# Handing out seven steps of the first weights' conversion in each early turn of an attention loop, not four

## The chip, the cores and the metric

The kernel runs on one core of a Trainium2 chip. The metric is the device time of one execution in microseconds (us). TensorE (PE in the profile) does matrix products and transposes, VectorE (DVE) and ScalarE (ACT) the elementwise work, GpSimd (POOL) a few additions, and SyncE (SP) issues the transfers between device memory and on-chip memory, all on one queue (q1).

## The reference

Three layers follow each other. The first is attention over q, k and v (2 batches, 8 heads, 576 positions, 64 wide), the sum of two softmax attentions: a pooled one, over means of four positions and repeated four times, and a local one with the mask |i - j| < 4. Its output is laid out as x, 1152 tokens by 512. The second is `g @ w_out` with `g = s * relu(x @ w_in)**2 + b`, 2048 wide; its weights arrive as float64 (1,024 KB for a quarter block of 128 x 1024 values). The third is a sum over four experts of `p[:, e] * (relu(x @ w1[e]) @ w2[e])`, 1024 wide, with normalised p.

    out = expert_layer(mlp(attention(q, k, v)))

## The kernel before, in words

**Units and turns.** Attention is cut into 16 units u (`NU`): four groups of (batch, half of the sequence) with four pairs of heads each. The loop at line 991 makes 19 turns i. Each turn calls eight functions (list at 979), each for the unit i minus a lag: `b_step` (lag 1: scores, maxima, exponentials), `a_step` (lag 0: transposes of k and q), `k_step`, `d_step` (lag 3: product with v), `c_step` (lag 2: transposes of the probabilities), `x_step` (lag 3: splits the result into a high part `xs[0]` and a low part `xs[1]`), `norm_step` (lag 1) and `v_step`. At a turn's end SP gets the loads: k and q for unit i+2 (lines 1021 and 1022), v4 and v for unit i. `unit u` is written u0, u1, ... below; unit u's scores are made in turn u+1.

**The first weights' conversion.** The first MLP's weights come as 64-bit words and are turned into two 32-bit parts, w0 and w1. For a quarter block these are six steps (line 207): `magnitude` (ACT, L157), `clamp` (DVE, L161), `join` (DVE, L167 and L175), `sign` (DVE, L186), `high` (ACT, L196) and `low` (DVE, L199), the last two after the next quarter's first steps have begun. `low` also issues the next raw load (L122) into one of two buffers. In turn 2 the four quarters of block 0 (24 steps) go into the list `side`: two of the first matrix, two of the second. They are called #1 to #4 here; #5 and #6, the first two of block 1, go into the list in turn 12. `side_step` takes one step from the list. The loop calls it after `b_step`, `k_step`, `c_step` and `v_step`; code that needs a quarter which isn't ready (`w1_ap`, `w2_ap`) calls it until it is.

**The dense products.** When a group's fourth unit is through `x_step` (u3 in turn 6), the first layer's products of that group go into `slots` and come out one or two a turn. All their matmuls have line 316.

**What sets the order.** The functions are called in the order of the text, but a scheduler then arranges each engine's instructions by readiness in its own model and by the order in which they were issued; only GpSimd keeps the text's order. On the chip every engine works its list in order. So the four matmuls of a dense product that need only the first pair of heads stand on PE in turn 4, long before the others. Where PE would idle in the first four units, `keep_warm` (L352) adds matmuls on zeros.

The functions that the change touches:

Of the kernel before, what the change touches and what calls it, by code (L numbers as in the profile page):

```python
# [22 lines left out]
def attn_moe_moe_kernel(  # L23
# [76 lines left out]
    def load_next():  # L100
        if not stream:
            return
        n, which, half = stream.pop(0)
        wi, wo, f0 = blocks[n]
        m = 2 if n < n_moe1 else 1
        dt = I32 if n < n_moe1 else F32
        if n < n_moe1:
            wi, wo = wi.bitcast(I32), wo.bitcast(I32)
        f0 += half * 256
        if which == 0:  # L110
            src = wi[:, f0 * m : (f0 + 256) * m].rearrange("(k p) f -> p k f", p=P)
        else:
            src = wo[f0 : f0 + 256, :].rearrange("(c p) d -> p c d", p=P)
        if n < n_moe1:
            t = rawp.tile([P, 2048], dt, tag="raw", name="raw")
        else:
            if "raw2" not in pools:
                t = rawp.tile([P, 2048], dt, tag="raw", name="raw2")
                pools["raw2"] = [t[:, :1024], t[:, 1024:]]
            t = pools["raw2"].pop(0)  # L120
            pools["raw2"].append(t)
        nc.sync.dma_start(out=t.rearrange("p (a b) -> p a b", a=src.shape[1]), in_=src)  # L122
        raw[n, which, half] = t
# [205 lines left out]
    def make_mask(t, m):  # L329
        if t == 0:  # L330
            nc.gpsimd.memset(mask, 0.0)
        off = t * TQ - window(t) if t <= MX else S - TQ - window(NTQ - 1)
        for sgn in (1, -1):
            nc.gpsimd.affine_select(
                out=mask[:, t : t + m],
                in_=mask[:, t : t + m],
                compare_op=ALU.is_ge,
                fill=NEG,
                base=FAC - 1 + sgn * off,
                pattern=[[0, m], [-sgn, W]],  # L340
                channel_multiplier=sgn,
            )
# [18 lines left out]
    def load_small():  # L361
        nc.sync.dma_start(out=s_sb, in_=s_in.rearrange("(o n) -> o n", o=1).to_broadcast([P, 1]))
        nc.sync.dma_start(out=b_sb, in_=b_in.rearrange("(o n) -> o n", o=1).to_broadcast([P, 1]))
        nc.sync.dma_start(out=pr, in_=probs.rearrange("(t p) e -> p t e", p=P))

    def norm_probs():
        nc.vector.tensor_reduce(out=prs, in_=pr, axis=AX.X, op=ALU.add)
        nc.vector.tensor_scalar(out=prs, in0=prs, scalar1=1e-9, scalar2=None, op0=ALU.add)
        nc.vector.reciprocal(out=prs, in_=prs)
        nc.vector.tensor_tensor(  # L370
            out=pr, in0=pr, in1=prs.to_broadcast([P, NT // P, E]), op=ALU.mult
        )
# [41 lines left out]
    def load_v4(u):  # L414
        if u < NU and unit(u)[3] == 0:
            g, j, b, hf = unit(u)
            v4 = ap4.tile([ND, 2, 2, FAC * D], F32, tag="v4", name="v4")
            nc.sync.dma_start(
                out=v4.rearrange("n a c f -> n (a c) f"),
                in_=v[b, 2 * j : 2 * j + 2].rearrange(  # L420
                    "a (c n r) d -> n (a c) (r d)", c=2, r=FAC
                ),
            )
            loaded["v4", u] = v4

    def load_k(u):
        if u < NU and unit(u)[3] == 0:
            g, j, b, hf = unit(u)
            kn = ap4.tile([KP, KR, 2, D], F32, tag="kn", name="kn", bufs=3)
            nc.sync.dma_start(  # L430
                out=kn, in_=k[b, 2 * j : 2 * j + 2].rearrange("a (p r) d -> p r a d", r=KR)
            )
            loaded["k", u] = kn

    def load_q(u):
        if u < NU:
            g, j, b, hf = unit(u)
            n0, m = tiles(hf)
            gd = m * TQ // FAC
            qn = ap2.tile([MX * TQ // FAC, FAC, 2, D], F32, tag="qn", name="qn")  # L440
            nc.sync.dma_start(
                out=qn[:gd],
                in_=q[b, 2 * j : 2 * j + 2, n0 * TQ : (n0 + m) * TQ, :].rearrange(
                    "a (n r) d -> n r a d", r=FAC
                ),
            )
            loaded["q", u] = qn

    def load_v(u):
        if u < NU:  # L450
            g, j, b, hf = unit(u)
            n0, m = tiles(hf)
            vn = ap2.tile([W, MX, 2, D], F32, tag="vn", name="vn", bufs=3)
            edge = 0 if hf == 0 else m - 1
            k0 = window(n0 + edge)
            nc.sync.dma_start(
                out=vn[:, edge],
                in_=v[b, 2 * j : 2 * j + 2, k0 : k0 + W, :].rearrange("a w d -> w a d"),
            )
            for a in range(2):  # L460
                t = 1 - hf
                s = v[b, 2 * j + a, window(n0 + t) :, :]
                nc.sync.dma_start(
                    out=vn[:, t : t + m - 1, a],
                    in_=bass.AP(s.tensor, s.offset, [[D, W], [TQ * D, m - 1], [1, D]]),
                )
            st["v", u] = vn
# [475 lines left out]
    def l1_steps(n, g):  # L943
        hs = hidden[n, g] = []
        if n < n_moe1:
            return [lambda fc=fc: moe1_l1(n, g, fc, hs) for fc in range(FC)]

        def run(half, i):
            if i == 0:
                hidden["steps"] = moe2_l1(n, g, half, hs)  # L950
            hidden["steps"][i]()

        return [lambda half=half, i=i: run(half, i) for half in range(2) for i in range(4)]

    def l2_steps(n, g):
        if n < n_moe1:
            return [lambda dc=dc: moe1_l2(n, g, dc, hidden[n, g]) for dc in range(KD)]
        t0, m = PARTS[g]
        return [
            lambda i=i: moe2_l2(n, t0 // P + i, i * P, hidden[n, g]) for i in range(2 * m // P)  # L960
        ]

    def side_step():
        if side:
            side.pop(0)()
        elif tail:
            tail.pop(0)()
# [23 lines left out]
    for i in range(last + 1):  # L991
        if i == 1:
            make_mask(CUT, 2)
            make_mask(MX + 1, 1)
        if i == 2:
            side += prep(0, 0, 0) + prep(0, 0, 1) + prep(0, 1, 0) + prep(0, 1, 1)
        if i == NU - 1:
            norm_probs()
        if i == NU - NP:
            rctx.close()  # L1000
            pools["wx"] = ctx.enter_context(
                tc.tile_pool(name="wx", bufs=1, side="right", reuse_waits="tile")
            )
            side += prep(1, 0, 0) + prep(1, 0, 1)
        for f, lag in steps:
            u = i - lag
            if 0 <= u < NU:

                with tc.high_priority(30) if f is a_step and u < NP else nullcontext():
                    f(u)  # L1010
            if f is x_step and u >= 0 and u % NP == NP - 1:
                slots += l1_steps(0, u // NP) + l2_steps(0, u // NP)
                if u < NP:

                    for _ in range(3):
                        slots.pop(0)()
            if f in (k_step, c_step) and slots and i < last:
                slots.pop(0)()
            if f in (b_step, k_step, c_step, v_step):
                side_step()  # L1020
        load_k(i + 2)
        load_q(i + 2)
        load_v4(i)
        load_v(i)
        if i == 4:
            load_small()
        if i < 2:
            load_next()
# [102 lines left out]
```

## Time and profile before

| what | value |
|---|---|
| runs | 702.38, 702.8 and 710.17 us, median 702.8 |
| span of the profiled execution | 709.2 us, first to last instruction |
| what lies around the span | not shown; the longest run is 1.0 above it |
| mean granted clock of the profiled execution | 0.969 |
| PE busy | 695.4 us, 98% of the span |
| DVE, ACT, POOL busy | 414.6, 347.8, 104.4 us |

The profiled execution's own time is not among the numbers; its span is 6.4 us above the median of the runs and 1.0 us below the longest, so it resembles the long one. Times of rows are from the span's start.

### The profile page before, as it was taken

The numbers are of one execution on the slowest core, as the hardware profiler recorded it, in microseconds if no ns is written. First come the engines' busy times: TensorE is split into PE (matmuls) and PEld (weight loads), VectorE is DVE, ScalarE is ACT, GpSimd is POOL, SyncE is SP. The second block draws the span as 40 slices with busy tenths as digits, with TensorE's granted clock in tenths as the row PEclk, the third lists the DMA queues.
The fourth block names the chain that finished last, engine by engine and source line by source line (L and its number), as shares of the span: only waits on it lengthen the run. The fifth ranks groups of instructions, "written<-read, shape, count | busy, mean of one in ns | idle before, by whom it ended". The sixth has DMA issues, their size and how long they took to land.

```text
span 709.2 us, 11407 instructions
## 1 busy us (share of the span) xinstructions
PE 695.4 (98%) x4496; PEld 633.9 (89%) x4496; DVE 414.6 (58%) x738; ACT 347.8 (49%) x854; POOL 104.4 (15%) x125
## 2 busy tenths in 40 slices
PE   8799989999999999999999999999999999999997
PEld 6678878899999999999989989899899898999996
DVE  3684987768894432579453555636645556365432
ACT  4553857768696565775454423423324244234220
POOL 5410244020000200103021021201210212010000
PEclk9855999999999999999999999999999999999999
DMA  9743644531540010200110110201102102011012
GB/s 182 197 116 95 119 85 105 132 125 63 175 146 34 1 30 0 60 2 30 30 61 30 60 30 30 64 27 60 60 30 60 30 31 64 26 56 35 1 55 79
DMA packets 54165, 46.39 MB, mean 65 GB/s; under 512 B 32224, under 2 KB 42720, under 8 KB 54112
## 3 DMA queue, kind: packets, MB, share of 16 engines
q1 hardware_dynamic: 54112, 45.67, 23.5%
q8 instruction: 35, 0.57, 0.3%
q14 instruction: 18, 0.15, 0.1%
HBM read 43.31 MB, written 2.36 MB: 64 GB/s over the span
## 4 chain that ended last, share of the span: by engine, by line
PE 88%; DVE 6%; ACT 3%; DMA 1%; issue 1%; POOL 0%; ACTq 0%; DVEq 0%
PE psm L316 41%; PE psx L864 25%; PE psx L316 13%; PE psa L598 2%; PE psa L686 2%; PE psa L658 1%; PE psa L352 1%; PE psa L616 1%; DMA qn<-in_q_dram 1%; PE psa L679 1%; PE psa L510 1%; DVE pd L636 1%; ACT pl L584 1%; DMA kn<-in_k_dram 1%; PE psa L492 1%
## 5 line engine op out<-in xcount | busy, mean ns | idle before, releaser
L316 PE MATMUL psm<-w,h 128*128 128x512 f32 x864 | 208.7, 391 | 0.0
L316 PEld LDWEIGHTS psm<-w,h 128*128 128x128 f32 x864 | 158.5, 188 | 30.0
L864 PE MATMUL psx<-x,w 128*128 128x320 f32 (+1 forms) x768 | 117.7, 296 | 0.0
L864 PEld LDWEIGHTS psx<-x,w 128*128 128x128 f32 x768 | 109.2, 189 | 1.7
L259 POOL TENSOR_TENSOR sw<-raw 128x256 f32<-128x256 f32 x32 | 31.3, 998 | 409.8 <-DMA raw<-in_moe_w_dram 292.0
L879 ACT COPY r<-psx 128x320 f32<-128x320 f32 (+1 forms) x96 | 38.1, 397 | 92.9 <-PE psx L864 92.5
L882 ACT ACTIVATE h<-r 128x320 fp32r<-128x320 f32 (+1 forms) x96 | 42.1, 444 | 83.5 <-DVE r L893 83.5
L935 DVE SCALAR_TENSOR_TENSOR acc<-psm,pr,acc 128x512 f32<-128x512 f32 x63 | 47.2, 749 | 57.9 <-PE psm L316 57.9
L864 PE MATMUL psx<-t,w 128*128 128x320 f32 (+1 forms) x448 | 80.2, 302 | 0.2 <-DVE r L893 0.2
L316 PE MATMUL psm<-x,w 128*128 128x320 f32 (+2 forms) x420 | 74.7, 329 | 4.6 <-ACT x L714 1.8
L893 DVE TENSOR_TENSOR r<-psx,r 128x320 f32<-128x320 f32 (+1 forms) x96 | 43.2, 456 | 58.3 <-PE psx L864 56.3
L316 PEld LDWEIGHTS psm<-x,w 128*128 128x128 f32 x420 | 67.6, 204 | 7.3 <-ACT x L714 2.1
L864 PEld LDWEIGHTS psx<-t,w 128*128 128x128 f32 x448 | 67.0, 188 | 4.5 <-DVE r L893 0.5
L883 DVE SCALAR_TENSOR_TENSOR h<-r,h 128x320 fp32r<-128x320 f32 (+1 forms) x96 | 48.1, 506 | 18.5 <-ACT h L882 16.4
L316 PE MATMUL psm<-h,w 128*128 128x256 f32 (+2 forms) x360 | 57.2, 305 | 0.5 <-ACT w L196 0.4
L316 PE MATMUL psx<-h,w 128*128 128x384 f32 (+1 forms) x312 | 55.8, 327 | 0.0
L316 PEld LDWEIGHTS psm<-h,w 128*128 128x128 f32 x360 | 50.8, 190 | 2.1 <-issue 1.1
L316 PEld LDWEIGHTS psx<-h,w 128*128 128x128 f32 x312 | 52.0, 188 | 0.0
L316 PE MATMUL psx<-x,w 128*128 128x384 f32 (+2 forms) x252 | 43.1, 320 | 0.0
L316 PEld LDWEIGHTS psx<-x,w 128*128 128x128 f32 x252 | 40.6, 188 | 0.0
L237 DVE TENSOR_TENSOR w<-raw,w 128x1024 fp32r<-128x1024 f32 x16 | 19.5, 1224 | 25.6 <-ACT w L234 25.6
L781 DVE TENSOR_TENSOR h<-r,h 128x384 fp32r<-128x384 f32 (+2 forms) x40 | 21.6, 541 | 19.9 <-ACT h L780 18.8
(109 smaller groups left out, 901.5 us busy)
## 6 DMA issues: line engine op xcount, KB each, us to landing
raw<-in_moe_w_dram SPq DMA_DIRECT2D x32, 512.0 KB
raw<-in_moe_w_in_dram SPq DMA_DIRECT2D x8, 1024.0 KB
raw<-in_moe_w_out_dram SPq DMA_DIRECT2D x8, 1024.0 KB
kn<-in_k_dram SPq DMA_DIRECT2D x8, 288.0 KB
v<-in_v_dram SPq DMA_DIRECT2D x8, 288.0 KB
out_dram<-acc SPq DMA_DIRECT2D x9, 256.0 KB
qn<-in_q_dram SPq DMA_DIRECT2D x8, 160.0 KB
vn<-in_v_dram SPq DMA_DIRECT2D x16, 72.0 KB
```

What stands on the lines that cost most here:

```text
L237: nc.vector.tensor_tensor(out=k0[1], in0=source(), in1=f32(k0[0]), op=ALU.subtract)
L259: nc.gpsimd.tensor_tensor(out=operand(out), in0=operand(x), in1=operand(y), op=op)
L316: nc.tensor.matmul(o, stat(ps, kk), mov(pm, kk, i), start=c == 0, stop=c == len(terms) - 1)
L598: nc.tensor.matmul(ps[0][:, t * W : t * W + W], qz[:, t].rearrange("p a q -> p (a q)"), kT[:, k0 : k0 + W], start=False, stop=t == m - 1,)
L686: nc.tensor.matmul(ps[o, t * TQ : t * TQ + TQ], vn[:, t, a], pT[:, i : i + TQ], start=True, stop=True,)
L781: nc.vector.tensor_tensor(out=h[1], in0=r, in1=f32(h[0]), op=ALU.subtract)
L864: nc.tensor.matmul(ps, s_ap(n, half, a, w, kk), xt[x, pi][b][:, kk], start=first and c == 0, stop=c == len(terms) - 1, skip_group_check=True,)
L879: nc.scalar.copy(t, st[name])
L882: nc.scalar.activation(out=h[0][:, halves[hf]], in_=t, func=ACTF.Relu)
L883: nc.vector.scalar_tensor_tensor(out=h[1][:, halves[hf]], in0=t, scalar=0.0, in1=f32(h[0][:, halves[hf]]), op0=ALU.max, op1=ALU.subtract,)
L893: nc.vector.tensor_tensor(out=st[t], in0=st[name], in1=st[t], op=ALU.add)
L935: nc.vector.scalar_tensor_tensor(out=a, in0=ps, scalar=p_e, in1=a, op0=ALU.mult, op1=ALU.add)
```

## The change

`side_step` is also called after `a_step`, `norm_step` and `d_step`, in the turns 0 to 6. The list is filled in turn 2, so up to seven steps leave it in each of the turns 2 to 5, and it is empty after the third step of turn 5; before, the last step left it in turn 7. No instruction of the computation is added or taken away.

```diff
-            if f in (b_step, k_step, c_step, v_step):
+            if f in (b_step, k_step, c_step, v_step) or (i < 7 and f in (a_step, norm_step, d_step)):
                 side_step()
```

What the scheduler makes of it shows on three engines. First DVE in turns 5 and 6; `cv` is a quarter's work buffer (before: cv_561 is #3; after: cv_466 is #3, cv_535 is #4), `qz1` the scaled q of u5, `md` a maximum of u4's pooled scores, `xg` the attention result of u2. Before:

```order
L618 TENSOR_REDUCE md_585<-psa_586 80x1
L199 TENSOR_TENSOR w01_286<-cv_399,w00_285 128x1024
L161 TENSOR_SCALAR cv_561<-cv_561 128x1024
L167 TENSOR_SCALAR cv_561<-cv_561 128x1024
L175 SCALAR_TENSOR_TENSOR cv_561<-raw_485,cv_561 128x1024
L524 TENSOR_SCALAR qz1_109<-psa_607 64x5x64
L539 TENSOR_REDUCE qd_614<-psa_607 128x80
L702 TENSOR_TENSOR xg_638<-psa_619,ud_636 128x256
L631 TENSOR_SCALAR sum0_106<-sum0_106 128x7
L186 SCALAR_TENSOR_TENSOR cv_561<-raw_485,cv_561 128x1024
```

and of the change:

```order
L618 TENSOR_REDUCE md_601<-psa_602 80x1
L161 TENSOR_SCALAR cv_466<-cv_466 128x1024
L167 TENSOR_SCALAR cv_466<-cv_466 128x1024
L175 SCALAR_TENSOR_TENSOR cv_466<-raw_404,cv_466 128x1024
L631 TENSOR_SCALAR sum0_106<-sum0_106 128x7
L186 SCALAR_TENSOR_TENSOR cv_466<-raw_404,cv_466 128x1024
L161 TENSOR_SCALAR cv_535<-cv_535 128x1024
L632 RECIPROCAL sum0_106<-sum0_106 128x7
L167 TENSOR_SCALAR cv_535<-cv_535 128x1024
L199 TENSOR_TENSOR w11_288<-cv_466,w10_287 128x1024
L175 SCALAR_TENSOR_TENSOR cv_535<-raw_495,cv_535 128x1024
L524 TENSOR_SCALAR qz1_109<-psa_623 64x5x64
```

Between the maximum and `qz1` stood four conversion instructions; now there are eight, and #2's L199 has moved ahead of the maximum.

Second SP, the loads at the end of turn 3; `raw` is a quarter (raw_404 is #3, raw_495 is #4), `qn` the q of u5. Before:

```order
L122 DMA raw_485<-in_moe_w_out_dram 128x2x1024
L441 DMA qn_487<-in_q_dram 80x8x64
L418 DMA v4_489<-in_v_dram 72x4x256
L456 DMA vn_491<-in_v_dram 72x2x64
L463 DMA vn_491<-in_v_dram 72x3x64 x2
```

and of the change:

```order
L122 DMA raw_404<-in_moe_w_out_dram 128x2x1024
L122 DMA raw_495<-in_moe_w_out_dram 128x2x1024
L441 DMA qn_497<-in_q_dram 80x8x64
L418 DMA v4_499<-in_v_dram 72x4x256
L456 DMA vn_501<-in_v_dram 72x2x64
L463 DMA vn_501<-in_v_dram 72x3x64 x2
```

Raw load #4, which waits for #2's L186 to free its buffer, now stands ahead of u5's q.

Third PE in turn 4, in one piece of the difference; x_76 is the high part of x, x_77 the low part, L610 the pooled scores of u3.

```order
 L316 MATMUL psm<-x_76,w_283 128x256 x2
-L316 MATMUL psm<-x_77,w_283 128x256 x2
-L316 MATMUL psm<-x_76,w_284 128x256 x2
-L610 MATMUL psa<-kd_435,qd_111 128x144
+L610 MATMUL psa<-kd_442,qd_111 128x144
+L316 MATMUL psm<-x_77,w_283 128x256
+L316 MATMUL psm<-x_76,w_284 128x256
+L316 MATMUL psm<-x_77,w_283 128x256
+L316 MATMUL psm<-x_76,w_284 128x256
 L510 MATMUL psa<-ident,qn 128x80 x4
```

u3's pooled scores no longer stand behind the matmuls that need the low part.

## Rows read from the trace of the kernel before

**Rows 1.** Stretches of the span: busy us of each engine, granted clock, transfers.

```profile
0.00:30.20 30.20, 25.31 (x188) 18.16 (x188) 15.94 (x39) 16.50 (x55) 13.31 (x30) 1.00 0.96 196
30.20:71.20 41.00, 38.81 (x215) 31.98 (x215) 24.39 (x50) 18.16 (x62) 6.81 (x7) 0.50 0.42 110
71.20:105.40 34.20, 31.70 (x310) 27.65 (x309) 30.66 (x57) 25.66 (x90) 13.36 (x13) 1.00 0.55 106
105.40:108.80 3.40, 3.40 (x15) 3.23 (x15) 1.17 (x5) 1.90 (x11) 0.08 (x1) 0.50 0.47 129
...
135.00:300.00 165.00, 165.00 (x1120) 162.72 (x1120) 101.99 (x157) 113.31 (x233) 10.84 (x11) 1.00 0.21 69
```

**Rows 2.** PE in order of time, turns 4 to 7: start, us, instruction, idle before.

```profile
29.96 0.55 PE L316 MATMUL psm<-x,w 128*128 128x256 f32 x2 [0.89 <-ACT x L714]
31.46 1.22 PE L316 MATMUL psm<-x,w 128*128 128x256 f32 x4 [0.94 <-POOL x L716]
...
42.61 2.07 PE L316 MATMUL psm<-x,w 128*128 128x256 f32 x8
45.93 1.22 PE L316 MATMUL psm<-x,w 128*128 128x256 f32 x4 [1.25 <-DVE w L199]
46.95 0.73 PE L510 MATMUL psa<-ident,qn 80*128 80x80 f32 x4
...
52.87 2.41 PE L598 MATMUL psa<-kT,qz 128*128 128x72 f32 x10
...
67.79 4.30 PE L316 MATMUL psm<-x,w 128*128 128x256 f32 x21
```

**Rows 3.** DVE in order of time, turns 4 to 6.

```profile
29.39 0.30 DVE L636 TENSOR_TENSOR pd<-pd,sum 128x144 f32<-128x144 f32 x1
...
42.76 1.39 DVE L636 TENSOR_TENSOR pd<-pd,sum 128x144 f32<-128x144 f32 x1
44.07 0.29 DVE L618 TENSOR_REDUCE md<-psa 80x1 f32<-80x144 f32 x1
44.29 1.58 DVE L199 TENSOR_TENSOR w<-cv,w 128x1024 fp32r<-128x1024 f32 x1
48.50 0.49 DVE L524 TENSOR_SCALAR qz<-psa 64x320 f32<-64x320 f32 x1
```

**Rows 4.** Conversion instructions by line, to 130 us: shortest, median, longest ns.

```profile
L161 DVE TENSOR_SCALAR cv<-cv x6: 674/687/1223, 22.2 to 90.2; 128x1024 f32<-128x1024 f32 x6
L167 DVE TENSOR_SCALAR cv<-cv x6: 676/690/1040, 23.6 to 92.0; 128x1024 int32<-128x1024 int32 x6
L175 DVE SCALAR_TENSOR_TENSOR cv<-raw,cv x6: 1209/1226/1330, 24.4 to 92.7; 128x1024 int32<-128x1024 int32 x6
L186 DVE SCALAR_TENSOR_TENSOR cv<-raw,cv x6: 1173/1217/1556, 25.7 to 95.2; 128x1024 int32<-128x1024 int32 x6
L199 DVE TENSOR_TENSOR w<-cv,w x6: 1206/1216/1582, 29.6 to 129.5; 128x1024 fp32r<-128x1024 f32 x6
```

**Rows 5.** SP's issues in order of time: start, us, transfer.

```profile
40.40 0.38 SPq L122 DMA_DIRECT2D raw<-in_moe_w_out_dram  x1
```

**Rows 6.** The whole span's chain in order of time: start, us, what.

```profile
17.51 6.06 DMA qn<-in_q_dram
```

**Rows 7.** DVE's groups by line, 72 to 110 us: count, busy us, mean ns.

```profile
L186 DVE SCALAR_TENSOR_TENSOR cv<-raw,cv 128x1024 int32<-128x1024 int32 x3 | 3.9, 1315 | 0.0
...
L199 DVE TENSOR_TENSOR w<-cv,w 128x1024 fp32r<-128x1024 f32 x2 | 2.4, 1216 | 0.1
```

**Rows 8.** PE in order of time, turns 8 to 11: what it waited for.

```profile
79.48 0.50 PE L316 MATMUL psm<-h,w 128*128 128x256 f32 x2 [0.41 <-ACT w L196]
...
97.18 1.00 PE L316 MATMUL psm<-x,w 128*128 128x320 f32 x5 [0.58 <-POOL x L716]
...
99.17 0.51 PE L610 MATMUL psa<-kd,qd 128*128 128x144 f32 x2 [0.32 <-DVE ml L606]
```

**Rows 9.** The chain from 85 to 100 us, shares by line.

```profile
by line: DVE cv L186 17.1%; issue 11.6%; DVE pd L636 11.1%; DVE pl L633 10.0%; DVE w L199 7.6%; PE psa L598 7.0%; DVE ml L606 5.6%; DVE qd L531 5.4%; PE psm L316 5.0%; DVE cv L161 4.0%; DVE md L618 3.6%; PE psa L610 3.5%; DVE xg L702 3.3%; 
```

## The prediction

> **What bounds the kernel now.** I first read the busy times by stretch [rows 1]. From 135 to 300 us PE is busy in all 165.0 us, and later nearly so; a step that leaves this work alone can change the time only by what PE loses before 135 us. That loss has two kinds. Idle: 4.9 us before 30.2, 2.2 us from 30.2 to 71.2, 2.5 us from 71.2 to 105.4. And clock: from 30.2 to 71.2 us the granted clock is 0.50, the lower level, 1.2 GHz, and again for 3.4 us from 105.4. PE had been busy 25.3 of 30.2 us when it fell, and was in a run of 21 dense matmuls when it rose [rows 2]. In that slow stretch PE is the bound: 38.8 of 41.0 us busy, DVE only 24.4. From 71.2 to 105.4 it is close: PE 31.7 and DVE 30.7 of 34.2. The order of time [rows 2, 3] then tells which instruction PE or DVE stands at, and the chain [rows 9] what is late in the second stretch.
>
> **What is added and removed.** Nothing: 24 conversion steps before and after, with the same DMAs. They leave the list up to two turns earlier. That the edit changes nothing is excluded, since the lists above differ on PE, DVE and SP.
>
> **Turn 4.** #1's L199 now runs ahead of u0's `xg`, so x comes one L199 later, 1.22 us [rows 4]. PE, which waited 0.89 us for it already, gets to its first two dense matmuls 1.22 us later, at 31.18. L610 goes next and no longer stands behind the low part of x; the four matmuls behind it follow at once if that part takes as long as its mean, or wait on. Bounds for PE at L510 of u4: +0.4 with the 0.94 us wait for the low part hidden behind L610's half microsecond, +0.9 with none of it. I take +0.65, between them; nothing in the rows is nearer to one.
>
> **Turn 5.** #2's L199 moves ahead of L633, L636 and the second L618. Before, PE waited 1.25 us for it between eight and four dense matmuls [rows 2]; now it is done some 1.3 to 1.6 us after the first L618, while PE is still in the eight. That wait goes: -1.25. PE's L510 of u5 stands at 46.95 + 0.65 - 1.25 = 46.35.
>
> **Turn 6, the cost.** The price is on DVE, ahead of `qz1` (L524). The second L618 ended at 44.36 [rows 3]; in the change it waits for +0.65 and for L199, 1.22 to 1.58, so it ends near 46.5 (46.2 to 46.6). Then come, by the medians of [rows 4]: L161 0.69, L167 0.69, L175 1.23, L186 1.22 for #3, L161 0.69 and L167 0.69 of #4, L199 1.22 of #3, L175 1.23 of #4, and two of L631 and L632 that I estimate at 0.2 each. Sum 8.06 us, to 54.56, and L524 itself 0.49: 55.05. The matmuls of u5's scores (L598) need it. PE would be there 52.87 - 46.95 = 5.92 us after L510, at 52.27. It waits 2.8 us, and starts 2.2 us later than before (52.87). Bounds: L636 took 1.39 us here and 0.30 a turn earlier [rows 3]; at 0.30 the cost is +1.1. With the longest durations of [rows 4] for all eight, 2.7 us more in sum, it is +4.8. I take +2.1, near the medians; L636 comes at nearly the same time as before, so its 1.39 is the nearer row.
>
> The raw load #4 and, behind it, u5's q are on SP: #4 is freed by #2's L186, which ended just before 40.40 [rows 5]. u5's q is issued about 0.4 us later. An earlier q load that was issued right behind a raw load took 6.06 us in the chain [rows 6], so this one lands near 46.9, 0.5 us after PE wants it. That is hidden: PE has 2.8 us to spare before DVE lets it go on.
>
> [...]
>
> The other loads that stand behind #4, #5 and #6 (v4 and vn of u3, later q and vn of u6 and u7) are used a turn or more later, and I cost them at nothing; that cover is PE's slow turns of some 12 us, and it shrinks where the clock is high.
>
> **Turns 6 and 7.** From there PE's list is as before, and DVE has slack again (24.4 of 41.0 us busy). PE arrives at the 21 dense matmuls at 67.79 + 2.1 = 69.9.
>
> **Turns 8 to 11, the gain.** Before, #4, #5 and #6 were converted between 71 and 97 us: three each of L161, L167, L175 and L186, and two of L199 [rows 7], by the medians of [rows 4] some 14 us of DVE. #4 is now done by turn 6 and #5 half done, so about 8 us leave that stretch. The chain runs through just these lines [rows 9] (L186 17.1%, L199 7.6%, L161 4.0%). But PE worked on meanwhile, and only its idle time can come back. The waits that end on conversion or on DVE's lateness are 0.41 (#4's L196), 0.58 and 0.32 [rows 8]: 1.3 us. The rest of the 2.5 us ends on latency between engines and I leave it. The 3.4 us of half clock from 105.4 cost 1.7; I leave them too. Bounds: nothing comes back, 0, or all of it, 2.5 + 1.7 = 4.2.
>
> **The sum.** +2.1 - 1.3 = +0.8 us. Against the profiled execution that is a span of 710.0. But that execution is a long one, 6.4 us above the median of 702.8. I put the sum on the median: 703.6, 703.5 in round numbers. With the bounds of the two terms, +1.1 - 4.2 = -3.1 to +4.8 - 0 = +4.8, it is 699.7 to 707.6. What makes executions of before differ by 7.4 us the rows don't show; the nearest that could is the half-clock stretch, where 7.4 us are 15 us of half clock.
>
> **Rivals.**
> *The clock helps (chance 0.25).* The wait between the eight and the four dense matmuls is what goes, so twelve run unbroken, 3.3 us. If this brings the clock back in turn 5, and DVE still holds PE until 55, PE's 15 us from 55 to 70 run at full clock and give back up to 7.5 us. For: the clock came back in a run of 21, and again at 108.8 us with PE busy in all of 105.4 to 108.8 [rows 1]. Against: the 2.8 us wait that follows lets it fall again, and the short executions may have had this gain before. With them at the median, what is left is the gain of turns 8 to 11 at its upper end: 702.8 + 1.1 - 4.2 = 699.7; with both, about 697.
>
> *The q load is late (0.10).* If u5's q takes twice the 6.06 us, it lands at 53, PE waits 6.6 us at L510 and reaches the scores at 58.9 instead of 52.87: +6.0 - 1.3, 707.5. It decides once q lands after 49.2, when the 2.8 us are used up. Against: 1 MB and 160 KB took the 6.06 us.
>
> *The clock hurts (0.20), the slower side.* The 2.8 us wait in turn 6 stands right before the nine dense matmuls of that turn. Where the clock came back there in the short executions, it no longer does, and most executions are of the long kind: 710.2 + 0.8 = 711. It decides when PE idles over 2 us ahead of L598 with the clock at either level. For: at 30.2 us the clock fell after a stretch with PE idle for 4.9 us in all. Against: I see no short execution.
>
> **The numbers.** Forecast 0.45, rivals 0.25, 0.10, 0.20. The time is that of the forecast, 703.5. The forecast's own range is 699.7 to 707.6; down to 697 and up to 711 it takes in most of the rivals, and about 2 in 10 lie outside. 2%, about what a measurement of this kernel can tell from no change, is 14 us: below 688.7 or above 716.9. No case ends there alone; below, the helpful clock together with every bound, 0.03; above, the long kind with a longer half-clock stretch as well, 0.06.
>
> **What would show it.** In the profile of the change: PE waits 2 to 3 us ahead of u5's L598 for DVE (right) or not at all (the cost is wrong); no wait for #2's L199 among the dense matmuls of turn 5; conversion instructions of #4 gone from 70 to 81 us; PE idle of 71 to 105 us down from 2.5 to about 1.2. The forecast is wrong if the half-clock stretch has another length than 41 us plus 2, or if new ones appear: each 2 us of it count as 1.

## The result and the profile after

| | before | after |
|---|---|---|
| median of 20 runs each | 702.97 us | 707.28 us |
| lowest and highest | 698.62, 712.49 | 705.43, 711.52 |
| ratio after to before | | 1.0088, 95% interval 1.0070 to 1.0106 |
| span of the profiled execution | 709.2 | 707.1 |

The change costs 4 to 6 us: 4.3 us, 0.6%, between the medians, and 0.9% by the ratio, which leaves out executions more than 1.5% above the fastest of their kernel. That is within 2% and within the range by 0.3 us, 3.8 us above the forecast. The two profiled executions, read alone, say the opposite: the one of after is 2.1 us the shorter. That contradiction is what the experiments had to solve.

The stretches of the profile after (start and end, length, busy us of PE, PEld, DVE, ACT and POOL with counts, granted clock, busy share of the DMA engines and GB/s) answer to [rows 1]:

```profile
0.00:30.20 30.20, 25.14 (x186) 18.00 (x186) 16.08 (x38) 16.07 (x54) 13.51 (x29) 1.00 0.93 199
30.20:50.70 20.50, 19.67 (x118) 16.50 (x119) 15.62 (x27) 12.63 (x38) 6.40 (x6) 0.50 0.39 113
50.70:54.10 3.40, 0.95 (x7) 0.48 (x5) 3.34 (x5) 0.37 (x1) 0.00 (x0) 1.00 1.09 309
54.10:74.60 20.50, 19.94 (x101) 16.61 (x101) 14.12 (x29) 10.61 (x35) 1.56 (x1) 0.50 0.64 118
74.60:105.40 30.80, 30.00 (x306) 26.86 (x306) 22.14 (x51) 22.26 (x89) 10.43 (x13) 1.00 0.34 75
105.40:108.80 3.40, 3.40 (x45) 3.04 (x43) 3.00 (x7) 3.10 (x11) 1.11 (x2) 1.00 0.50 134
```

The clock comes back at 50.7 us, 20 us earlier than in the profiled execution of before, and finds PE standing still: 0.95 us busy of 3.4. It falls again, for another 20.5 us. So the half-clock time is 41.0 us, as in the one long stretch of before, but in two pieces, and the dip of 3.4 us at 105.4 is gone.

PE after, in order of time (start, us, instruction, count, idle before it and what ended that), answers to [rows 2]:

```profile
30.97 0.80 PE L316 MATMUL psm<-x,w 128*128 128x256 f32 x2 [2.03 <-ACT x L714]
...
32.90 0.73 PE L510 MATMUL psa<-ident,qn 80*128 80x80 f32 x4
...
42.55 2.93 PE L316 MATMUL psm<-x,w 128*128 128x256 f32 x12
45.54 0.80 PE L510 MATMUL psa<-ident,qn 80*128 80x80 f32 x4
...
53.71 2.08 PE L598 MATMUL psa<-kT,qz 128*128 128x72 f32 x10 [2.45 <-DVE qz L524]
```

The 1.25 us wait between eight and four dense matmuls is gone (x12 unbroken), and 2.45 us stand ahead of u5's scores instead. DVE after, answering to [rows 3], shows where they come from:

```profile
42.19 1.21 DVE L199 TENSOR_TENSOR w<-cv,w 128x1024 fp32r<-128x1024 f32 x1
...
43.91 0.30 DVE L618 TENSOR_REDUCE md<-psa 80x1 f32<-80x144 f32 x1
44.12 0.68 DVE L161 TENSOR_SCALAR cv<-cv 128x1024 f32<-128x1024 f32 x1
...
51.92 1.21 DVE L175 SCALAR_TENSOR_TENSOR cv<-raw,cv 128x1024 int32<-128x1024 int32 x1
53.16 0.49 DVE L524 TENSOR_SCALAR qz<-psa 64x320 f32<-64x320 f32 x1
```

From 44.12 to 53.13 us DVE has nothing but the eight conversion instructions of #3 and #4 and two small ones; then comes L524. SP after, answering to [rows 5]:

```profile
26.82 13.06 SPq L122 DMA_DIRECT2D raw<-in_moe_w_out_dram  x2
39.94 0.60 SPq L441 DMA_DIRECT2D qn<-in_q_dram  x1
```

SP stands 13 us at the second raw load (#4), and u5's q goes out behind it, at 39.94. Before, u5's q went out right behind raw load #3, 12.95 us ahead of #4 [rows 5]:

```profile
26.96 0.39 SPq L122 DMA_DIRECT2D raw<-in_moe_w_out_dram  x1
27.45 0.60 SPq L441 DMA_DIRECT2D qn<-in_q_dram  x1
```

### The profile page after: what moved, and what is told of

It is laid out like the page before. It is cut to its first block, busy times and chain, and to the rows that moved or that the text cites. A ratio compares the mean times of both kernels' runs of the same rounds, so it can differ in the third digit from the quotient of the medians.

```text
span 707.1 us, 11409 instructions
## 1 busy us (share of the span) xinstructions
PE 693.3 (98%) x4496; PEld 632.9 (89%) x4496; DVE 414.8 (59%) x738; ACT 348.4 (49%) x854; POOL 102.4 (14%) x125
## 4 chain that ended last, share of the span: by engine, by line
PE 91%; DVE 5%; ACT 2%; issue 1%; POOL 0%; ACTq 0%
PE psm L316 42%; PE psx L864 25%; PE psx L316 13%; PE psa L598 2%; PE psa L658 2%; PE psa L686 2%; PE psa L352 1%; PE psa L616 1%; PE psa L679 1%; PE psa L510 1%; PE psa L492 1%; DVE cv L161 1%; DVE w L199 0%; PE psa L589 0%; DVE ts L836 0%
```

## The experiments

**What every run tells.** Each run lists its span and mean granted clock, so its half-clock time can be worked out as 2 x (1 - clock) x span. Against the stretches read from the traces this is off by up to 2 us (15.5 against 13.6 us in `after_warm8`). The profiled execution of before gives 44 us. That number is used below.

**1. Before again, and parts of the change.** `same` is the kernel before, to catch a short execution. `six` and `five` leave calls out:

```diff
-            if f in (b_step, k_step, c_step, v_step) or (i < 7 and f in (a_step, norm_step, d_step)):
+            if f in (b_step, k_step, c_step, v_step) or (i < 7 and f in (norm_step, d_step)):   # six
+            if f in (b_step, k_step, c_step, v_step) or (i < 7 and f is d_step):                # five
```

Expected of `same`:

> The kernel before, unchanged, to see one of its short executions. Theory 1 (eight conversion instructions ahead of unit 5's qz, and PE's 2.45 us wait there, are the loss) and theory 2 (#1's L199 ahead of unit 0's xg is the loss) say only that its median is near 703. Theory 3 (the clock): if the profile catches an execution of about 700 us, its half-clock stretches before 135 us sum to some 26 to 31 us instead of the 41.0 + 3.4 us of the 709.2 us span, and the clock comes back around turn 5 or 6 and doesn't fall again; if the sum is 41 us or more in a short execution, theory 3 is wrong.

Of `six`:

> Steps are handed out also behind norm_step and d_step, not behind a_step: #1's L199 still runs ahead of unit 0's xg and #2's L199 early, as in the change, but only three conversion instructions (L161, L167, L175 of #3) stand ahead of unit 5's qz, not eight. Theory 1: PE's 2.45 us wait for L524 is gone or under 0.5 us, and the median is 700 to 703. Theory 2: the 2.03 us wait for x in turn 4 stays and the median stays at about 707. Theory 3: the clock does not fall again in turn 6, some 27 to 38 us at half clock, 699 to 704.

Of `five`:

> Steps are handed out also behind d_step alone: #2's L199 is early, #1's L199 stays behind unit 0's xg as before, and no clump stands ahead of unit 5's qz. Theory 1: no wait for L524, the 1.25 us wait in turn 5 is gone, 701 to 702. Theory 2: the same 701 to 702, since turn 4 is as before; so if six is at 707 and this one at 702, theory 2 holds, and if both are near 702, theory 1. Theory 3: as six, 699 to 704, with some 27 to 38 us at half clock.

Measured: `same` 701.12 us; `six` 701.98 us, ratio to before 1.0020 (0.9989 to 1.0052); `five` 702.35 us, 1.0031 (1.0017 to 1.0046). `five` ran once more under the label five_warm8 (its keep-warm matmuls are four, in spite of the label): 703.33 us.

> Steps handed out also behind d_step alone, once more, one look: as in the first run of it, half clock of 20 to 28 us in two stretches, about 702.

Its half-clock time came in three stretches, 23.8 us in all, not in two.

The profile of `same` caught a short execution, span 701.1 us. Its stretches:

```profile
28.70:52.60 23.90, 21.89 (x125) 17.70 (x125) 16.48 (x27) 11.50 (x38) 6.78 (x7) 0.50 0.54 141
52.60:97.00 44.40, 41.55 (x398) 35.91 (x398) 38.18 (x79) 31.85 (x114) 12.99 (x14) 1.00 0.56 118
97.00:100.40 3.40, 3.40 (x14) 3.04 (x15) 1.36 (x4) 1.56 (x10) 0.71 (x1) 0.50 0.36 94
```

Here too the clock comes back in turn 6, at 52.6 us, but PE is in u5's scores then and has no wait above 0.42 us until 72: it stays up for 44 us. So the two kinds of executions of before differ by the clock: of 47 (12 of `same`, 35 of before beside it) 35 have 7 to 27 us of half clock, with a median time of 700.9 us, and 12 have 44 us, with 710.3. Per microsecond of half clock that is 9.5 / 27 = 0.35 us, less than the half that PE alone would lose; that a faster PE waits more would explain it, but was not tried. All 20 executions of after have 30 to 42 us: the short kind is gone. `six` has 24 to 31 (27 to 38 expected), `five` 21 to 28.

The clock doesn't tell the whole time. Three of the 35 take 709 us with 21 us of half clock. And in after three executions with 31 us take 711 us, the longest of all, while those with 41 to 42 us take 707 to 709. No profile caught one of these, and what makes them longer is open.

Theory 2 falls: `six` keeps the 2.03 us wait for x in turn 4 and is 5 us faster than the change. What `six` lacks is the clump ahead of L524:

```profile
31.72 0.51 PE L316 MATMUL psm<-x,w 128*128 128x256 f32 x2 [2.03 <-ACT x L714]
...
46.84 1.23 DVE L175 SCALAR_TENSOR_TENSOR cv<-raw,cv 128x1024 int32<-128x1024 int32 x1
48.10 0.49 DVE L524 TENSOR_SCALAR qz<-psa 64x320 f32<-64x320 f32 x1
...
49.33 1.33 PE L598 MATMUL psa<-kT,qz 128*128 128x72 f32 x10
```

L524 starts 5.06 us earlier than in the change, and PE does not wait for it. `six` lacks the late load as well, so it can't tell the two apart: u5's q goes out ahead of raw #4.

```profile
28.07 0.60 SPq L441 DMA_DIRECT2D qn<-in_q_dram  x1
39.71 0.39 SPq L122 DMA_DIRECT2D raw<-in_moe_w_out_dram  x1
```

**2. More keep-warm work in units 0 to 3.**

```diff
-    fill = [4 if u < NP else 0 for u in range(NU)]
+    fill = [8 if u < NP else 0 for u in range(NU)]
```

As `before_warm8` and, with the change, `after_warm8`:

> The kernel before with eight keep-warm matmuls, not four, in each place of units 0 to 3: PE has less idle time up to 30 us. Theory 3: the clock falls later than 30 us or comes back earlier than 71 us, and the time falls by half of what the half-clock stretch loses: 10 us less of it gives 5 us, about 698, less the keep-warm matmuls' own time where PE is the bound (some 160 more rows of matmuls). Theories 1 and 2 expect no gain from it: 703 to 706, the keep-warm work being only added.

> The change with eight keep-warm matmuls, not four, in each place of units 0 to 3, as the run before_warm8 had them, whose median was 698.2 with 4 us of half clock in most executions. Theory 3: with the clock up in turns 4 and 5, PE comes to unit 5's scores earlier and waits 4 us or more for the eight conversion instructions; either the clock falls there (some 10 to 20 us of half clock, 701 to 706), or it stays and what is left is idle time, 698 to 700. Theory 1 without the clock: 2 to 3 us above before_warm8, 700 to 701. If the handing out as such were good once the clock is high: 697 or less.

Measured: `before_warm8` 698.24 us, ratio 0.9964 (0.9932 to 0.9996), half clock 0 to 14 us, median 4, with 80 keep-warm matmuls more (168 for 88); `after_warm8` 706.29 us, half clock 7 to 24, median 17 (5.1 above the median of the before beside it; the ratio, 1.0026 with 0.9983 to 1.0069, takes in no change, so the traces are compared). Useless matmuls make before faster; with them, the change costs 8 us between the medians. Stretch 27 to 75 us of both, before first:

```profile
27.00:75.00 48.00, 45.63 (x451) 39.02 (x450) 42.10 (x88) 35.63 (x128) 12.93 (x11) 1.00 0.66 150
```

```profile
27.00:75.00 48.00, 43.30 (x367) 35.64 (x368) 41.72 (x76) 30.82 (x104) 11.72 (x9) 0.86 0.66 152
```

Between the profiled spans, 704.4 and 696.5, lie 7.9 us. The half clock is 13.6 us in the one and 3.4 in the other, worth 5.1 at most; PE's idle time is 2.3 us more in this stretch. PE's waits after (27 to 75 us: in total, times, longest) show one that the profile of the change did not have:

```profile
PE psa L510 <- DMA qn<-in_q_dram: 2.2, 1, 2.2
...
PE psa L598 <- DVE qz L524: 0.6, 1, 0.6
```

With the clock up, PE is at L510 of u5 before the q load has landed. The 4 us or more that were expected ahead of L598 are 0.6, since PE has lost 2.2 at the transposes before it.

**3. Filling the wait.** Twelve more keep-warm matmuls right ahead of u5's scores (`after_fill`), or behind u6's transposes (`after_late`):

```diff
-            keep_warm(ps, n, fill[u])
+            keep_warm(ps, n, 16 if u == 3 and not cols else fill[u])   # after_fill
-        keep_warm(psq, m * TQ, fill[u])
+        keep_warm(psq, m * TQ, 12 if u == 6 else fill[u])              # after_late
```

> The change, with twelve more keep-warm matmuls of 128x256 right ahead of unit 5's scores, where PE waits 2.45 us for L524. The lists of DVE, SP and POOL are those of the change, and L524 comes at the same time. Theory 3 (PE's idle time in turn 6 lets the clock fall again, and the second half-clock stretch of 20.5 us is the loss): the wait shrinks to about 0.5 us or less, the clock does not fall at 54, some 20 us of half clock are left in all instead of 41, and the median falls by 6 to 10 us to 697 to 701 though only useless work was added. Theory 1 in its narrow form (the late scores themselves are the loss, the clock has nothing to do with it): the same 707.

> A control: the change, with twelve more keep-warm matmuls of 128x192 behind unit 6's transposes, after the wait for L524 and in the second half-clock stretch. Theory 3: the 2.45 us wait stays, the clock falls at 54 as in the change, and the median is 707 to 710, up to 12 x 0.16 = 1.9 us of added work at half clock. If keep-warm matmuls help wherever they stand, 697 to 703.

Measured: `after_fill` 707.06 us (ratio 1.0029, 0.9983 to 1.0075), half clock 17 to 38, median 28; `after_late` 707.29 us (1.0078, 1.0037 to 1.0119). Theory 3 in the narrow form missed: the wait for L524 fell to 0.76 us, the half clock by 7.7 us between the medians, and the time stayed. L598 still starts when DVE lets it, and the matmuls cost their own time. The control's time is as expected. L598 of `after_fill`:

```profile
51.79 1.33 PE L598 MATMUL psa<-kT,qz 128*128 128x72 f32 x10 [0.76 <-DVE qz L524]
```

But both profiled executions are of another kind than that of the change, though the lists are the same up to the added matmuls. PE's waits of `after_late`, 27 to 75 us:

```profile
PE psa L598 <- DVE qz L524: 2.6, 1, 2.6
PE psm L316 <- ACT x L714: 2.0, 1, 2.0
PE psa L510 <- DMA qn<-in_q_dram: 1.9, 1, 1.9
```

and its stretches, with the clock:

```profile
29.90:36.70 6.80, 6.30 (x46) 5.83 (x47) 3.51 (x8) 3.74 (x14) 2.69 (x3) 0.50 0.17 66
36.70:47.00 10.30, 7.05 (x67) 5.56 (x66) 10.20 (x19) 7.31 (x21) 1.83 (x2) 1.00 0.58 161
47.00:60.70 13.70, 10.85 (x50) 8.24 (x48) 11.69 (x17) 5.26 (x15) 3.72 (x3) 0.50 1.00 221
```

The clock is back at 36.7 us already, PE is idle for 3.25 of the next 10.3 us, the longest part waiting for u5's q, and the clock falls at 47. So there are two waits, one behind the other: q for the transposes, and L524 for the scores. Whichever level the clock has, one of them or both find PE.

**4. Where u5's q stands on SP.** The theory was widened to cover both waits. The scheduler works by readiness in its own model; with q behind raw #4 it would count on it late, and put L524, which needs it, behind conversion that is ready sooner. (Only the orders that come of it can be seen, not the model's reasons.) `after_q` raises that one load's priority and leaves the hand-out as in the change:

```diff
-        load_q(i + 2)
+        with tc.high_priority(60) if i == 3 else nullcontext():
+            load_q(i + 2)
```

> The change, with only unit 5's q load raised in priority, so that it stands on SP ahead of raw loads #3 and #4 instead of behind #4; the scheduler then also puts qz (L524) of unit 5 ahead of #3's and #4's conversion on DVE, with no conversion instruction between the second L618 of turn 5 and it. All steps are handed out as in the change. Theory 1, widened (the change makes u5's q late behind raw #4, and with it u5's qz late behind eight conversion instructions): PE waits neither for q at L510 of unit 5 nor for L524, and the median falls by 4 to 7 us, to 700 to 703, with 20 to 28 us of half clock. If the early hand-out itself or turn 4's delay is the loss: 706 or more.

> The same with eight keep-warm matmuls, not four, in each place of units 0 to 3. after_warm8 was at 706.3, before_warm8 at 698.2. Widened theory 1: without the late q and the late qz the 8 us between those two go, and the median is 696 to 700. If the loss sits elsewhere in the early hand-out: 704 or more.

Measured: `after_q` 703.24 us, ratio 1.0009 (0.9979 to 1.0038), an interval that lies wholly below the change's; half clock 21 to 35, median 24. `after_q_warm8` 700.99 us, 0.9979 (0.9948 to 1.0011), half clock 7 to 17. Between the medians 4.0 and 5.3 us come back (3.0 and 6.1 with each run beside its own before) by raising the priority of one load of 160 KB. Both medians still lie above the ranges expected, by 0.2 and 1.0 us, and `after_q_warm8` is 2.75 us above `before_warm8`. SP, DVE and PE of `after_q`:

```profile
24.94 1.44 SPq L441 DMA_DIRECT2D qn<-in_q_dram  x1
27.57 12.55 SPq L122 DMA_DIRECT2D raw<-in_moe_w_out_dram  x2
...
44.16 0.49 DVE L524 TENSOR_SCALAR qz<-psa 64x320 f32<-64x320 f32 x1
...
41.78 0.79 PE L510 MATMUL psa<-ident,qn 80*128 80x80 f32 x4
...
48.70 1.33 PE L598 MATMUL psa<-kT,qz 128*128 128x72 f32 x10
```

Both waits at u5 are gone. The raised load moves more than itself: L524 now starts 9 us earlier than in the change, and PE's twelve dense matmuls of turn 5 stand in pieces behind u5's transposes, not ahead of them. `six`, which is at least as fast, keeps those twelve ahead (42.66 us), so the gain does not need them moved; the late load and the late L524 are not separated by any run. `after_q` is not free of waits; the conversion now stands ahead of another short instruction, in turn 6:

```profile
PE psa L658 <- DVE pd L636: 2.4, 1, 2.4
```

`no_a3` takes away one early call only, `a_step`'s in turn 3 (`and not (i == 3 and f is a_step)`), which lets u5's q go ahead of raw #4 and puts u6's behind #4 and #5:

> The change without one of its early calls, the one behind a_step in turn 3. The lists then have u5's q ahead of raw #4 and three conversion instructions ahead of u5's qz, but u6's q behind both raw #4 and raw #5 on SP, and seven conversion instructions (L161, L167, L175, L186 of #3, L161 of #4, L199 and the rest behind) ahead of u6's qz, a turn later. Widened theory 1: PE waits no more at unit 5, and waits for DVE or for q at unit 6 instead; the place where it waits moves with the q load, and the time lies between after_q and the change, 702 to 707. If the early hand-out as such were the loss, the wait at unit 5 stays. If turn 6 has so much cover that u6's late q costs nothing, 700 to 703, as six and five.

Measured: 704.76 us, ratio 1.0051 (1.0017 to 1.0086), between `after_q` and the change, though its interval overlaps both. The wait for q went with the load. SP, then PE in turns 5 and 6:

```profile
27.20 0.60 SPq L441 DMA_DIRECT2D qn<-in_q_dram  x1
...
39.05 0.39 SPq L122 DMA_DIRECT2D raw<-in_moe_w_out_dram  x1
48.57 0.39 SPq L122 DMA_DIRECT2D raw<-in_moe_w_in_dram  x1
49.01 0.59 SPq L441 DMA_DIRECT2D qn<-in_q_dram  x1
...
43.03 0.44 PE L510 MATMUL psa<-ident,qn 80*128 80x80 f32 x4
...
47.29 1.33 PE L598 MATMUL psa<-kT,qz 128*128 128x72 f32 x10 [0.91 <-DVE qz L524]
...
55.18 0.77 PE L510 MATMUL psa<-ident,qn 80*128 80x80 f32 x4 [1.47 <-DMA qn<-in_q_dram]
```

u5's transposes wait for nothing, u6's for q. That PE would not wait at u5 at all is missed: its scores still wait 0.91 us for L524, behind three conversion instructions.

**5. Is there a better version?** `five` with eight keep-warm matmuls (`d_warm8`):

> Steps handed out also behind d_step alone, with eight keep-warm matmuls in each place of units 0 to 3. Three conversion instructions stand ahead of unit 5's qz, and raw #4 stands on SP ahead of unit 5's q as in none of the runs with d_step alone so far is looked at yet. Theory 1, widened: 697 to 700 if q comes in time, 700 to 703 if PE waits for q at L510 of unit 5.

Measured: 701.71 us, ratio 0.9986 (0.9952 to 1.0021), half clock 3 to 18. That misses the 697 to 700 expected with q in time, though PE does not wait for q in its profile. The expectation had the order on SP wrong: u5's q goes out at 26.71 us and raw #4 at 39.05, behind it. The best kernel of all remains `before_warm8`, without any early hand-out.

## Why the prediction came out as it did

**Turn 4: +0.65 predicted, -0.05 measured.** L510 of u4 starts at 32.90, 32.95 before. x came late as predicted (PE waits 2.03 us), but L610 and the low part then followed without a wait. No loss, as `six` shows as well.

**Turn 5: -1.25 predicted, -1.36 measured** against like executions (45.54 - 46.95 + 0.05). The step is right.

**Turn 6: right in kind.** The wait of 2.8 us is 2.45. L618 ended at 44.21, not 46.5, since L636 took 0.30 us and not 1.39; the eight instructions took 9.0 us, not 8.1 (one L161 took 1.76 us). L598 starts 0.84 us later than before, not 2.2.

**The q load: 0.5 us late and hidden, predicted; true only where the clock is low.** In the profile of the change PE came to L510 at 45.54 and waited for nothing. The bound of the rival (it decides once q lands after 49.2) took PE's arrival from a profile at half clock; at full clock PE is there at about 43 us and waits 1.8 to 2.2 us. The load itself was priced well: issued at 39.38 in `after_late`, used at 44.94, 5.6 us against the 6.06 of [rows 6].

**Turns 8 to 11: -1.3 predicted, -3.0 measured** (u14's L589 stands at 132.02, 134.07 before, and the 21 dense matmuls began 0.96 us later). The idle time from 74.6 to 105.4 us is 0.8 us, and the dip of the clock at 105.4 is gone; both lie within the bounds given.

**The step that failed: "I put the sum on the median."** Against the long execution the sum is not +0.8 but -2.1. Against the median it is +4.3, because the median of before is made of short executions, and the change has none. The sum kept the long half-clock stretch as it was, without a term for what the new wait would do to it. That the time still lies inside the range, by 0.3 us, is luck: the upper end, 707.6, was made of the longest conversion durations. By the forecast's own sign, half-clock stretches that are new or of another length, it is wrong.

With the medians of all runs, the half clock rises from 18 us (the 47 executions of before) to 35. What that is worth hangs on the price. At one half it is 8.6 us, and what is left of the time falls by some 2.8; at the 0.35 us found above it is 6.0, and what is left falls by 0.9. The loss itself is 5.5 us between these medians, 4.3 beside the before of the same batch. So at either price the clock outweighs a saving of 1 to 3 us; this is a sum over medians, not a measurement of the clock alone.

The rival "the clock hurts" names this in the right place (the wait in turn 6), with a chance of 0.20 and a price of 711; executions with 41 to 42 us of half clock take 707 to 709. The rival "the clock helps" was right in its first half and in what it held against itself: the clock came back early, at 50.7 us, and fell again at 54.1, behind the wait. The rival of the late q adds its part in the executions with an early return of the clock.

**What stays open.** That the clock falls because of these waits is not shown. In several traces of the change and its variants a fall stands within 4 us behind a wait of 1.8 to 2.5 us (54.1 after, 47.0 in `after_late`). But in `before_warm8` PE waits 1.5 us at u5's scores and the clock stays, and in `six`, which has neither wait at u5, it falls all the same, at 53.7, for 13.6 us; the longest wait since its return at 46.8 is 0.93 us:

```profile
47.31 1.33 PE L598 MATMUL psa<-kT,qz 128*128 128x72 f32 x10 [1.51 <-DVE qz L524]
...
53.01 1.52 PE L316 MATMUL psm<-x,w 128*128 128x256 f32 x8 [0.93 <-POOL x L716]
```

(the first line is `before_warm8`, the second `six`). The Trainium skill (TensorE: Matmul & The Clock Gate, section HAM oscillation — how this bites in real kernels) tells of a matmul loop in which the wait for a transfer lets the clock fall in every tile. The fall at 47.0 behind the 1.9 us wait for q looks alike, but the waits told of there are longer, and the fall in `six` has no wait for a transfer ahead of it. `after_fill`, which was to show the link by filling one wait, did not make the kernel faster; the q wait stayed. Nor is it known why the first half-clock stretch is so different in length (6.8 us in `after_late`, 20.5 in the profile after, though it starts at 29.9 and 30.2 and the lists are the same up to there).

## What to carry to other kernels

A step that is handed out earlier takes its transfers along: look where the next small load stands behind a raw load on the queue, and what the scheduler then puts ahead of its consumer on another engine. Where the executions of a kernel fall into two kinds, a sum made against one trace holds for that kind only; list the granted clock of every run first, and put into the sum a term, or at least a rival with a price, for what the clock does there. And filler work on an idle PE can be worth more than earlier useful work on another engine: -0.4% against +0.9% here.

## What was not expected of the hardware

- One program, unchanged, ran with 7 to 44 us of half clock in 47 executions. Its times, 698 to 711 us, rise with it, except for three at 709 us with 21 us.
- Twice as many keep-warm matmuls in units 0 to 3 brought the half clock to 4 us in six of twelve executions and to 0 in one, for a gain of 3.7 us net between the medians.
- L161, 0.69 us at the median [rows 4], took 1.76 us in the clump, and L167 and L199 1.64 and 1.74 us in `after_late`; POOL was at work beside the first (L472). That the two are linked was not tried.
